# Scales from sums of squares in place of largest magnitudes, with the order of the work made anew, in an attention and MLP kernel

## Chip, cores and metric

The kernel runs on one core of a Trainium2 chip. The metric is the device time of one execution in microseconds (us). Before the change it is 663.16 us, the median of 3 runs (662.82 to 663.47).

## The reference

Eight batches of eight heads with 512 rows of x and 32 rows of state, 64 wide. x reads the state and the state reads x, each through a softmax. The 544 rows of each batch, 512 wide, then go through a layer norm and a two-layer MLP with a residual.

```
scores = x @ state.T / 8;      xread = softmax(scores) @ state
scores2 = state @ x.T / 8;     sread = softmax(scores2) @ x
x = concatenate([xread, sread]), heads side by side       # 8 x 544 x 512
xn = (x - mean) / sqrt(var + 1e-6) * g_ln
out = x + max(xn @ w_ch1, 0) @ w_ch2                      # 512 -> 2048 -> 512
```

The weights and g_ln reach the device as they are drawn; a weight comes as two 32-bit words a number.

## The kernel before

**Numbers as pairs.** Products are made in 16-bit floats, with each operand as a high and a low part (`hi`, `lo`) and three of the four cross products (`TERMS`). For that, each operand is first multiplied by a power of two that brings it into range. There are two scales for each batch (x and state, `x_s`, with the inverses `x_i`) and one for each of the four blocks of either weight (`of_weights`, inverses `is` and for w2 a column of `of_weights`).

**How a scale was found.** In `attention(b)` (L370) ScalarE takes magnitudes of a quarter of x with a running sum beside them (`AF.Abs`, L386), or VectorE a largest magnitude (`absmax`, L351, two quarters of batch 0 and the state's block `sj`); VectorE combines the four parts into `x_am`. `across` (L343) then crosses the partitions: TensorE transposes the column by the identity `idf`, VectorE reduces the row to `x_t`, TensorE spreads it over all partitions by a product with `ids`, and VectorE takes the result as `x_m`. `scales` (L332) keeps the exponent and takes a reciprocal. For a weight block `largest_square` (L607) makes the block's Gram matrix in 16 products of 128 columns, reduces it by its maximum, and goes through `across`; `scales_of_squares` (L337) halves the exponent.

**Weights.** `words` (L586) joins the two words of a number in place: ScalarE treats the high word (`Prelu`) and, for the first half of a block, the low one (`Copy`); for the second half VectorE shifts the low one; VectorE then joins both. For w1, `means` (L636) multiplies by g_ln/512 on TensorE, VectorE subtracts it (four operations `sums<-sums,gx,acc` or `raw<-raw,gx,acc`), then the block is scaled into `w1c` by `split` (L603: ScalarE the high, VectorE the low part). `weights2` does the same for `w2h` without the means.

**Batches.** Batch 0 goes through `first_products` (L730 in `multiply`) and `second_product` (L744) unit by unit while weights arrive: `scores` (L429), softmax on `ts`, numerators `ef` and `ea`, read of the state (L506), mixing (L551). `state_products` multiplies the state with w1 into `matrix` (L689). Batches 1 to 7 use seven products instead of eight per block (L828 the hidden rows into `half`, L886 the seven products into `acc`, with `together` for their sums); the state's rows come last (L838).

**Order.** Each of these is a stream of single operations, 178 in all, and the string `PLAN` lists in which order their operations are issued, as stream:operation. Each engine does its own in that order and waits for what it needs. The last stream, 177, is `WARM` = 119 products of a block of ones with itself into `half`, whose result nobody reads (L191, `half<-ones`); `PLAN` puts them among the first real products. `banks` is one double accumulator bank with a single buffer, shared by scores, reads, mixing, state products and the scales of x. Most operations carry L191, the line of the helper `do`.

Of the kernel before, what the change touches and what calls it, by code (L numbers as in the profile page):

```python
# [19 lines left out]
EXP_MASK = 0x7F800000  # L20
HALF_EXP_MASK = 0x3F800000
TINY = 1e-30
# [4 lines left out]
SX = 2.0**14  # L27
SE = 2.0**12
SA = 2.0**5
SN = 4.0  # L30
SW = 2.0**13
S2 = 2.0**12
CM = 2.0**-24
SB = 2.0**19
# [171 lines left out]
def moe_attention(ctx: ExitStack, tc: tile.TileContext, x, state, g_ln, w1, w2, out):  # L206
# [109 lines left out]
    nc.vector.tensor_tensor(fold, idf[:, 0:D], idf[:, D:2 * D], ALU.add)  # L316
    mhalf = tiny("mhalf", C)
    nc.vector.memset(mhalf, -0.5)

    ones = main.tile([P, P], BF16, name="ones")  # L320
    nc.vector.memset(ones, 1.0)  # L321

# [679 lines left out]
```

## Time and profile before

| | us |
|---|---|
| median of the runs | 663.16 |
| the profiled execution | 663.94 |
| its span, first to last instruction | 662.1 |
| VectorE busy in the span | 496.2 |
| ScalarE busy | 368.3 |
| GpSimd busy | 220.6 |

The mean granted clock of TensorE is 0.996. In the rows below, a timeline row has start, length, engine, line, operation, outputs and inputs, shapes and count, and in brackets how long the engine was idle before and what ended that. PEld is the loading of TensorE's stationary operand, which lies beside its products. A row of windows has the stretch, its length, and for each engine the busy time and the number of instructions.

### The profile page before, as it was taken

To read this page: it belongs to the slowest core of one execution; us is meant where nothing else is said; L and a number is where in the kernel's file an instruction comes from. 1 tells how busy PE (TensorE), PEld (TensorE's weight loads), DVE (VectorE), ACT (ScalarE), POOL (GpSimd) and SP (SyncE) were. 2 spreads that over 40 slices of the span, in tenths; PEclk is the share of its full clock that TensorE was granted. 3 is DMA by queue.
4 is the path that set the end of the run, shared out by engine and by line. 5 is a ranking of instruction groups with operands and counts; after the bars stand their busy time and mean duration, and the time that the engine had idled before them with its cause. 6 is when DMAs were issued, how large, how long until landed. Compare 5 with 4: busy or idle time off the path is not lost. (4 is left out here: it accounts for less than half of the span.)

```text
span 662.1 us, 15974 instructions
## 1 busy us (share of the span) xinstructions
PE 641.5 (97%) x6647; PEld 502.0 (76%) x6647; DVE 496.2 (75%) x990; ACT 368.3 (56%) x659; POOL 220.6 (33%) x189
## 2 busy tenths in 40 slices
PE   9999999999999999999999999999999999999995
PEld 4446646668878888778787888788788887888885
DVE  3999998667599689678785887699777966677424
ACT  4499886748535754466445553755475534444331
POOL 0014134412243335324431335326333442335122
PEclk9998999999999999999999999999999999999999
DMA  8897666331052551434152235340704213102001
GB/s 321 210 304 290 150 152 146 76 71 38 13 99 47 135 103 40 98 112 58 50 133 81 44 76 122 86 73 33 174 10 64 76 36 97 65 2 33 33 1 64
DMA packets 90040, 63.15 MB, mean 95 GB/s; under 512 B 69297, under 2 KB 82097, under 8 KB 89521
## 3 DMA queue, kind: packets, MB, share of 16 engines
q1 hardware_dynamic: 87696, 58.18, 34.2%
q0 software_dynamic: 864, 3.15, 2.5%
q8 instruction: 52, 0.85, 0.6%
q10 hardware_dynamic: 1408, 0.82, 0.4%
q14 instruction: 20, 0.16, 0.1%
HBM read 28.05 MB, written 9.44 MB: 57 GB/s over the span
## 5 line engine op out<-in xcount | busy, mean ns | idle before, releaser
L886 PEld LDWEIGHTS <-xs 128*128 128x128 f16 x2520 | 243.5, 98 | 41.3 <-issue 9.8
L191 POOL TENSOR_TENSOR xs<-rs,xs 128x512 f16<-128x512 f32 x120 | 142.0, 1195 | 291.5 <-ACT xs L191 189.5
L886 PE MATMUL acc<-w2h,xs 128*128 128x256 f16 x1440 | 182.2, 273 | 2.1 <-POOL xs L191 0.8
L828 PE MATMUL half<-ea,matrix 128*128 128x256 f16 x1344 | 162.5, 273 | 4.6 <-DVE xs L191 2.5
L828 PEld LDWEIGHTS <-matrix 128*128 128x128 f16 x1344 | 128.9, 98 | 27.1 <-issue 6.3
L886 PE MATMUL acc<-sums,xs 128*128 128x256 f16 x1080 | 142.6, 273 | 0.7 <-DVE strip L191 0.7
L191 DVE SCALAR_TENSOR_TENSOR rs<-half,rs 128x256 f32<-128x256 f32 x224 | 90.0, 418 | 36.2 <-ACT rs L191 15.7
L191 ACT ACTIVATE xs<-rs 128x512 f16<-128x512 f32 (+1 forms) x128 | 77.2, 620 | 69.6 <-DVE rs L191 58.7
L191 ACT ACTIVATE xs<-half 128x256 f16<-128x256 f32 (+1 forms) x112 | 53.4, 487 | 85.5 <-PE half L828 31.8
L191 DVE SCALAR_TENSOR_TENSOR xs<-half,xs 128x256 f16<-128x256 f32 (+1 forms) x112 | 61.2, 549 | 21.0 <-ACT xs L191 20.7
L744 PE MATMUL acc<-w2h,hid 128*128 128x512 f16 x192 | 44.8, 390 | 0.1
L191 DVE SCALAR_TENSOR_TENSOR matrix<-banks,hs,matrix 128x1024 f16<-128x1024 f32 x28 | 35.8, 1278 | 10.5 <-ACT matrix L191 10.3
L191 DVE TENSOR_TENSOR strip<-acc,strip 128x256 f32<-128x256 f32 (+1 forms) x60 | 33.1, 552 | 9.3 <-PE acc L886 7.0
L191 ACT ACTIVATE rs<-half 128x256 f32<-128x256 f32 x56 | 21.4, 381 | 32.2 <-PE half L828 27.3
L744 PEld LDWEIGHTS <-hid 128*128 128x128 f16 x192 | 18.7, 100 | 23.1 <-issue 3.0
L191 ACT ACTIVATE matrix<-banks,hs 128x1024 f16<-128x1024 f32 x28 | 31.1, 1110 | 5.7 <-PE banks L689 5.5
L191 POOL TENSOR_TENSOR hid<-strip,hid 128x512 f16<-128x512 f32 x16 | 22.4, 1415 | 25.2 <-ACT hid L191 23.6
L191 PE MATMUL half<-ones 128*128 128x512 bf16 x119 | 29.4, 399 | 1.1 <-DVE ones L321 1.1
L191 POOL TENSOR_TENSOR ts<-ts,mA 128x1024 f32<-128x1024 f32 (+1 forms) x8 | 14.7, 1842 | 40.2 <-DVE of_weights L191 28.9
L191 DVE SCALAR_TENSOR_TENSOR x<-x_f,x_s,x 128x512 f16<-128x512 f32 x32 | 26.9, 863 | 1.1 <-ACT x L191 1.0
L191 DVE BATCH_NORM_STATS2 s<-xr 128x6 f32<-128x512 f32 x32 | 21.8, 683 | 6.9 <-ACT xr L191 6.9
L191 DVE SCALAR_TENSOR_TENSOR xr<-strip,of_second,xr 128x512 f32<-128x512 f32 x28 | 24.6, 889 | 0.3
(149 smaller groups left out, 780.5 us busy)
## 6 DMA issues: line engine op xcount, KB each, us to landing
raw<-in_moe_w_ch_dram SPq DMA_DIRECT2D x10, 1024.0 KB, 7.1
out_dram<-xr SPq DMA_DIRECT2D x16, 512.0 KB, 2.9
x_f<-in_x_dram SPq DMA_DIRECT2D x15, 512.0 KB, 5.2
sums<-in_moe_w_ch_dram SPq DMA_DIRECT2D x6, 1024.0 KB, 7.1
ek<-ea SPq DMA_DIRECT2D x56, 64.0 KB, 2.1
ek<-ek SPq DMA_DIRECT2D x7, 512.0 KB, 4.4
xr<-part POOLq DMA_DIRECT2D x6, 512.0 KB, 5.1
s_r<-in_state_dram SPq DMA_DIRECT2D x28, 64.0 KB, 3.7
```

The source lines that it names most:

```text
L191: return lambda: f(*map(now, args), **{k: now(v) for k, v in kw.items()})
L744: nc.tensor.matmul(po, lhsT=hid[:, i, q, c * P:(c + 1) * P], rhs=w[:, j, q], start=first and q == 0 and n == 0, stop=last and q == 3 and n ...
L828: nc.tensor.matmul(ps[:, 256 * q:256 * q + 256], lhsT=m[:, h, i, P * (2 * k + q):P * (2 * k + q) + P], rhs=ea[:, 0, j, h, 256 * g:256 * g ...
L886: nc.tensor.matmul(po[o], lhsT=y[:, n, i, o] if o < 2 else x[:, o - 2, n, i], rhs=v[j], start=u == 0 and n == 0 and k == 0 and o in (2, 1, ...
```

## The change

The largest magnitude goes as a measure. ScalarE now squares each quarter of x, and the state's block from batch 1 on, with a running sum (`AF.Square`). In batch 0 VectorE still takes the largest magnitude of two quarters and of the state's block (`most`) and squares the three. The parts are 16-bit columns, `x_part`. Five products of `ones` with such a column (`totals`) give on all partitions the sum for x (four columns) and for the state (one). VectorE reads them and makes scale and inverse by integer arithmetic on the exponent, without a reciprocal. For a weight block the Gram matrix stays; its maximum goes into a 16-bit column `of_columns`, and one product with `ones` gives the total. Some constants change with it. In block 0 of both weights ScalarE also does the low words of the second half (`both`), which VectorE did. `WARM` is 102, and `PLAN` is another one throughout.

```
-    def scales(m, s, inv):
-        yield do(nc.vector.tensor_scalar, inv.bitcast(I32), m.bitcast(I32), EXP_MASK, None, ALU.bitwise_and)
-        yield do(nc.vector.reciprocal, s, inv)
-    def scales_of_squares(m, s, inv, c):
-        yield do(nc.vector.tensor_scalar, inv.bitcast(I32), m.bitcast(I32), 1, HALF_EXP_MASK, ALU.logical_shift_right,
+    def scales(total, m, s, inv, top):
+        yield do(nc.vector.tensor_scalar_max, m, total, TINY)
+        yield do(nc.vector.tensor_scalar, m.bitcast(I32), m.bitcast(I32), 1, HALF_EXP_MASK, ALU.logical_shift_right,
                  ALU.bitwise_and)
-        yield do(nc.vector.tensor_scalar, inv, inv, 2.0**64 / c, None, ALU.mult)
-        yield do(nc.vector.reciprocal, s, inv)
-    def across(a, n, i, m, t, ps):
-        yield do(nc.tensor.transpose, ps[0:n, 0:P], a, idf)
-        yield do(nc.vector.tensor_reduce, t[0:n], ps[0:n, 0:P], AX.X, ALU.max)
-        yield do(nc.tensor.matmul, ps[:, P:P + n], lhsT=t[0:n].broadcast_to([n, P]), rhs=ids[0:n, i, 0:n], start=True,
-                 stop=True)
-        yield do(nc.vector.tensor_scalar_max, m, ps[:, P:P + n], TINY)
+        yield do(nc.vector.tensor_scalar, s.bitcast(I32), m.bitcast(I32), -1.0, float((190 + top) << 23), ALU.mult, ALU.add)
+        yield do(nc.vector.tensor_scalar, inv.bitcast(I32), m.bitcast(I32), float((64 - top) << 23), None, ALU.add)
+    def totals(ps, parts):
+        for k, cols in enumerate(parts):
+            for n, c in enumerate(cols):
+                nc.tensor.matmul(ps[:, k:k + 1], lhsT=ones, rhs=c, start=n == 0, stop=n == len(cols) - 1)
...
-        for q in range(4):
-            v = xf.rearrange("p h c d -> p (h c) d")[:, 8 * q:8 * q + 8]
-            if b > 0 or q % 2 == 0:
-                yield do(nc.scalar.activation, x16[:, 8 * q:8 * q + 8].bitcast(BF16)[:, :, 0], v, AF.Abs,
-                         accum_out=part[:, q:q + 1])
-            else:
-                yield absmax(part[:, q:q + 1], v.rearrange("p a d -> p (a d)"))
-        yield absmax(am[:, 1:2], sj.rearrange("p g d -> p (g d)"))
-        yield absmax(am[:, 0:1], part)
+        for n, q in enumerate((0, 2) if b == 0 else range(4)):
+            yield do(squares, x16[:, 8 * q:8 * q + 8].bitcast(BF16)[:, :, 0], xq[q], part[:, n:n + 1])
+        if b > 0:
+            yield do(squares, sh.bitcast(BF16)[:, :, 0, 0], sj, part[:, 4:5])
+        else:
+            for n, v in enumerate((xq[1], xq[3], sj)):
+                yield do(nc.vector.tensor_reduce, most[:, n:n + 1], v.rearrange("p a d -> p (a d)"), AX.X, ALU.max,
+                         apply_absolute_value=True)
+            yield do(nc.vector.tensor_tensor, part[:, 2:5], most, most, ALU.mult)
...
-            if fh == 0:
+            if fh == 0 or both:
...
-        yield do(nc.vector.tensor_reduce, col, total[:, 0:P], AX.X, ALU.max)
-        yield from across(col, 1, 1, m, top, total[:, P:3 * P])
+        yield do(bound, col, total[:, 0:P])
+        yield do(lambda ps, c: totals(ps, ([c],)), total[:, P:P + 1], col)
...
-WARM = 119
+WARM = 102
```

Two engines' rows of the new order follow, at three places. At the scale of x in batch 0, TensorE has 35 products of `ones` ahead of the transpose by `idf`, two more ahead of the product with `ids`, and 28 behind it up to the first means. Now it has 30, the five products L347 `banks<-x_part,ones`, and 30.

The first place is VectorE's row from the first load of x to the scale of x. Before:

```order
L191 TENSOR_REDUCE x_part<-x_f 128x1
L191 TENSOR_REDUCE x_am<-s_j 128x1
L191 TENSOR_REDUCE x_part<-x_f 128x1
L191 TENSOR_REDUCE x_am<-x_part 128x1
L191 TENSOR_SCALAR gm<-gx 128x4
L191 TENSOR_REDUCE x_t<-banks 2x1
L191 TENSOR_SCALAR x_m<-banks 128x2
L191 TENSOR_SCALAR x_i<-x_m 128x2
L191 RECIPROCAL x_s<-x_i 128x2
L191 SCALAR_TENSOR_TENSOR sh<-s_j,x_s,sh 128x2x64
```

Now:

```order
L187 TENSOR_REDUCE most<-s_j 128x1
L187 TENSOR_REDUCE most<-x_f 128x1 x2
L187 TENSOR_TENSOR x_part<-most 128x3
L187 TENSOR_SCALAR gm<-gx 128x4
L187 TENSOR_SCALAR x_m<-banks 128x2
L187 TENSOR_SCALAR x_m<-x_m 128x2
L187 TENSOR_SCALAR x_s<-x_m 128x2
L187 SCALAR_TENSOR_TENSOR sh<-s_j,x_s,sh 128x2x64 x2
```

The state's block is reduced first, one reading of `banks` is gone, and the inverse `x_i` has moved behind the first parts of x.

The second place is ScalarE's row behind that scale (`x` is the pair of x, `sums` and `raw` hold weight words). Before:

```order
L191 ACTIVATE x_111<-x_f,x_s 128x8x64 x2
L191 ACTIVATE sh<-s_j,x_s 128x2x128
L191 ACTIVATE sums<-sums 128x1024
L191 ACTIVATE x_111<-x_f,x_s 128x8x64
L191 ACTIVATE sums<-sums 128x1024 x2
L191 ACTIVATE x_111<-x_f,x_s 128x8x64
L191 ACTIVATE sums<-sums 128x1024 x2
L191 ACTIVATE raw<-raw 128x1024
L191 ACTIVATE w1c<-sums,of_weights 128x2048
```

Now:

```order
L187 ACTIVATE sh<-s_j,x_s 128x2x128
L187 ACTIVATE x_113<-x_f,x_s 128x8x64 x4
L187 ACTIVATE sums<-sums 128x1024 x6
L187 ACTIVATE w1c<-sums,of_weights 128x2048
L187 ACTIVATE ts<-ts,es 128x512
```

The state's block comes first, the four quarters of x follow each other, and the word operations no longer stand between them; one of `raw` has moved behind `w1c`, and one on `sums` (`both`) has come.

The third is VectorE's row from the means of the first w1 block to its scale, with buffer numbers (`acc_236` and `acc_246` are that block's Gram, `acc_287` that of w2). Before:

```order
L191 SCALAR_TENSOR_TENSOR sums_70<-sums_70,gx_80,acc_218 128x512 x4
L191 SCALAR_TENSOR_TENSOR sums_70<-sums_70 128x1024
L191 SCALAR_TENSOR_TENSOR sums_70<-raw_159 128x1024
L191 TENSOR_REDUCE of_weights_277<-acc_236 128x1
L191 STREAM_TRANSPOSE ts_297<-banks_258 128x512
L191 TENSOR_REDUCE of_weights_277<-acc_236 1x1
L191 TENSOR_REDUCE of_weights_277<-acc_287 128x1
L191 TENSOR_SCALAR of_weights_277<-acc_236 128x1
L191 TENSOR_SCALAR is1_313<-of_weights_277 128x1
L191 TENSOR_SCALAR is1_313<-is1_313 128x1
L191 TENSOR_SCALAR es_316<-x_i_169 128x1
L191 RECIPROCAL of_weights_277<-is1_313 128x1
```

Now:

```order
L187 SCALAR_TENSOR_TENSOR sums_70<-sums_70 128x1024
L187 SCALAR_TENSOR_TENSOR sums_70<-sums_70,gx_80,acc_214 128x512 x4
L187 STREAM_TRANSPOSE ts_275<-banks_234 128x512
L342 TENSOR_REDUCE of_columns_277<-acc_246 128x1
L187 TENSOR_REDUCE mA_282<-ts_275 128x16
L187 TENSOR_SCALAR of_weights_284<-acc_246 128x1
L187 TENSOR_SCALAR of_weights_284<-of_weights_284 128x1 x2
L187 TENSOR_TENSOR ts_275<-ts_275,mA_282 128x512
L187 TENSOR_REDUCE mp_313<-banks_234 128x4
L187 TENSOR_TENSOR mB_315<-mp_313 128x2
L187 STREAM_TRANSPOSE ts_275<-banks_234 128x512
L187 TENSOR_SCALAR mB_315<-mB_315,es_227 128x2
```

One join of w2's words stands ahead of the means, the other has moved far behind; the work on w2's Gram is no longer mixed in; the low part of `w1c` is the next row, with less of the softmax ahead of it.

Behind the scale, TensorE has 16 products of `ones` ahead of the first state products (24 before). Then come 17 and 1 around twelve mixing products, and its first product with `matrix`; before, it had 7 and 8, with one set of means between them.

More of the change, by code (lines that the diff above doesn't have):

```diff
@@ L18 @@
 PSUM = bass.MemoryType.PSUM
-EXP_MASK = 0x7F800000
 HALF_EXP_MASK = 0x3F800000
@@ L26 @@
 SIGN_BIT = -(2.0**32)
-SX = 2.0**14
 SE = 2.0**12
-SA = 2.0**5
+SA = 2.0**3
 SN = 4.0
[L31 to L34, printed above, removed]
+CM = 2.0**-18
+SB = 2.0**15
 SR = 2.0**-6
@@ L318, in moe_attention @@
     nc.vector.memset(mhalf, -0.5)
+    most = tiny("most", 3)
     ones = main.tile([P, P], BF16, name="ones")
@@ L325, in moe_attention, with squares, bound @@
         nc.vector.tensor_scalar(signs[:, i], idf, 1.0 - 2.0 * i, None, ALU.mult)
-    ids = tiny("ids", 4).rearrange("p (a b) -> p a b", a=2)
-    for i, c in enumerate((SX, 1.0)):
-        nc.scalar.activation(ids[0:2, i], idf[0:2, 0:2], AF.Copy, scale=1.0 / c)
-    def scales(m, s, inv):
-        yield do(nc.vector.tensor_scalar, inv.bitcast(I32), m.bitcast(I32), EXP_MASK, None, ALU.bitwise_and)
-        yield do(nc.vector.reciprocal, s, inv)
-    def scales_of_squares(m, s, inv, c):
-        yield do(nc.vector.tensor_scalar, inv.bitcast(I32), m.bitcast(I32), 1, HALF_EXP_MASK, ALU.logical_shift_right,
-                 ALU.bitwise_and)
-        yield do(nc.vector.tensor_scalar, inv, inv, 2.0**64 / c, None, ALU.mult)
-        yield do(nc.vector.reciprocal, s, inv)
-    def across(a, n, i, m, t, ps):
-        yield do(nc.tensor.transpose, ps[0:n, 0:P], a, idf)
-        yield do(nc.vector.tensor_reduce, t[0:n], ps[0:n, 0:P], AX.X, ALU.max)
-        yield do(nc.tensor.matmul, ps[:, P:P + n], lhsT=t[0:n].broadcast_to([n, P]), rhs=ids[0:n, i, 0:n], start=True,
-                 stop=True)
-        yield do(nc.vector.tensor_scalar_max, m, ps[:, P:P + n], TINY)
-    def absmax(a, t):
-        return do(nc.vector.tensor_reduce, a, t, AX.X, ALU.max, apply_absolute_value=True)
+    def scales(total, m, s, inv, top):
+        yield do(nc.vector.tensor_scalar_max, m, total, TINY)
+        yield do(nc.vector.tensor_scalar, m.bitcast(I32), m.bitcast(I32), 1, HALF_EXP_MASK, ALU.logical_shift_right,
+                 ALU.bitwise_and)
+        yield do(nc.vector.tensor_scalar, s.bitcast(I32), m.bitcast(I32), -1.0, float((190 + top) << 23), ALU.mult, ALU.add)
+        yield do(nc.vector.tensor_scalar, inv.bitcast(I32), m.bitcast(I32), float((64 - top) << 23), None, ALU.add)
+    def squares(junk, v, total):
+        with nc.allow_low_precision(reason="bounds"):
+            nc.scalar.activation(junk, v, AF.Square, accum_out=total)
+    def bound(col, gram):
+        with nc.allow_low_precision(reason="bounds"):
+            nc.vector.tensor_reduce(col, gram, AX.X, ALU.max)
+    def totals(ps, parts):
+        for k, cols in enumerate(parts):
+            for n, c in enumerate(cols):
+                nc.tensor.matmul(ps[:, k:k + 1], lhsT=ones, rhs=c, start=n == 0, stop=n == len(cols) - 1)
     gm = tiny("gm", C)
@@ L380, in attention @@
         xf, sj, sr = tiles
-        am, part = column("x_am", 2), column("x_part", 4)
+        part = Later(lambda: small.tile([P, 16], BF16, name="x_part"))
         x16 = rows("x16").bitcast(F16).rearrange("p (a i d) -> p a i d", i=2, d=D)
-        for q in range(4):
-            v = xf.rearrange("p h c d -> p (h c) d")[:, 8 * q:8 * q + 8]
-            if b > 0 or q % 2 == 0:
-                yield do(nc.scalar.activation, x16[:, 8 * q:8 * q + 8].bitcast(BF16)[:, :, 0], v, AF.Abs,
-                         accum_out=part[:, q:q + 1])
-            else:
-                yield absmax(part[:, q:q + 1], v.rearrange("p a d -> p (a d)"))
-        yield absmax(am[:, 1:2], sj.rearrange("p g d -> p (g d)"))
-        yield absmax(am[:, 0:1], part)
+        xq = [xf.rearrange("p h c d -> p (h c) d")[:, 8 * q:8 * q + 8] for q in range(4)]
+        for n, q in enumerate((0, 2) if b == 0 else range(4)):
[7 more added lines that the diff above has]
+            yield do(nc.vector.tensor_tensor, part[:, 2:5], most, most, ALU.mult)
         m, sc, isc = column("x_m", 2), column("x_s", 2), column("x_i", 2)
-        yield from across(am, 2, 0, m, column("x_t"), banks()[:, 0])
-        yield from scales(m, sc, isc)
+        pt = banks()[:, 0, 0:2]
+        yield do(lambda ps, part: totals(ps, ([part[:, q:q + 1] for q in range(4)], [part[:, 4:5]])), pt, part)
+        yield from scales(pt, m, sc, isc, 14)
         sx, sst, isx, isst = sc[:, 0:1], sc[:, 1:2], isc[:, 0:1], isc[:, 1:2]
@@ L582, in moe_attention, with words @@
     is1 = Later(lambda: tiny("is1", U))
-    of_weights = Later(lambda: main.tile([P, 2 * U, 6], F32, name="of_weights"))
+    of_weights = Later(lambda: main.tile([P, 2 * U, 4], F32, name="of_weights"))
     uoq = Later(lambda: tiny("uoq", U))
-    def words(src, raws, t):
+    of_columns = Later(lambda: main.tile([P, 32], BF16, name="of_columns"))
+    def words(src, raws, t, both):
         for fh in range(2):
@@ L605, in split, with sum_of_squares @@
         yield do(engine.scalar_tensor_tensor, lo, t, s, hi, ALU.mult, ALU.subtract)
-    def largest_square(t, total, m, top, col):
+    def sum_of_squares(t, total, col):
         tops = t.bitcast(BF16).rearrange("p (e two) -> p e two", two=2)
@@ L631, in weights1 @@
         scale, m = of_weights[:, u, 0:1], of_weights[:, u, 2:3]
-        yield from words(src, raws, t)
+        yield from words(src, raws, t, u == 0)
         t4 = t.rearrange("p (k f) -> p k f", k=4)
@@ L641, in weights1 @@
             yield do(nc.vector.scalar_tensor_tensor, t4[:, k], t4[:, k], gx[:, k:k + 1], ps, ALU.mult, ALU.subtract)
-        yield from largest_square(t, accumulator(), m, of_weights[:, u, 3:4], of_weights[:, u, 1:2])
-        yield from scales_of_squares(m, scale, is1[:, u:u + 1], SW)
+        total = accumulator()
+        yield from sum_of_squares(t, total, of_columns[:, u:u + 1])
+        yield from scales(total[:, P:P + 1], m, scale, is1[:, u:u + 1], 13)
         yield from split(w[:, 0], w[:, 1], t, scale)
@@ L656, in weights2 @@
         w = wide(u, "w2h").bitcast(F16).rearrange("p (i q e) -> p i q e", i=2, q=4)
-        s, am, m, top, inv = (of_weights[:, U + u, k:k + 1] for k in range(5))
-        yield from words(src, raws, t)
-        yield from largest_square(t, accumulator(), m, top, am)
-        yield from scales_of_squares(m, s, inv, S2)
+        s, m, inv = (of_weights[:, U + u, k:k + 1] for k in range(3))
+        yield from words(src, raws, t, u == 0)
+        total = accumulator()
+        yield from sum_of_squares(t, total, of_columns[:, U + u:U + u + 1])
+        yield from scales(total[:, P:P + 1], m, s, inv, 12)
         yield do(nc.vector.tensor_scalar, uoq[:, u:u + 1], inv, is1[:, u:u + 1], None, ALU.mult)
```

244 rows, old and new, of the table PLAN are left out of this document.

## The prediction

> **What bounds the kernel now.** I read the page's shares first, then TensorE's busy time by stage, then the timeline of the first 60 us.
>
> ```profile
> PE 641.5 (97%) x6647; PEld 502.0 (76%) x6647; DVE 496.2 (75%) x990; ACT 368.3 (56%) x659; POOL 220.6 (33%) x189
> L191 PE MATMUL half<-ones 128*128 128x512 bf16 x119 | 29.4, 399 | 1.1 <-DVE ones L321 1.1
> ```
>
> TensorE is busy 97% of the span, but 29.4 us of it are the 119 fillers on `ones`, which compute nothing. The stages, cut where the last filler ends (45.06 us) and where the last product ends:
>
> ```profile
> 0.00:45.06 45.06, 42.13 (x236) 18.18 (x238) 32.41 (x66) 25.64 (x35) 3.13 (x8) 1.00 0.86 266
> 45.06:110.00 64.94, 63.08 (x605) 39.46 (x605) 61.26 (x115) 55.20 (x85) 20.36 (x17) 0.97 0.66 193
> 110.00:655.00 545.00, 535.92 (x5811) 444.27 (x5810) 399.53 (x807) 287.44 (x541) 197.07 (x165) 1.00 0.30 70
> ```
>
> The columns are the stretch, its length, busy us of PE, PEld, DVE, ACT and POOL, then clock and DMA. From 45 us on TensorE has real work nearly without a gap (idle 1.9 us up to 110, 9.1 us up to 655), and VectorE has 3.7 us to spare between 45 and 110. So two things can shorten the run: that the real products begin earlier, and that TensorE has less to do. The end behind 655 us holds no scale and is left as it is.
>
> **The start, step by step.** The timeline's rows that set it (start, length, engine, operation, what ended its wait):
>
> ```profile
> 7.36 0.29 DVE L191 TENSOR_REDUCE x_am<-s_j 128x1 f32<-128x128 f32 x1 [0.22 <-DMA s_j<-in_state_dram]
> 7.56 0.68 DVE L191 TENSOR_REDUCE x_part<-x_f 128x1 f32<-128x512 f32 x1
> 10.57 0.27 PE L191 MATMUL banks<-idf,x_am 128*2 128x128 f32 x1
> 11.30 0.35 PE L191 MATMUL banks<-ids,x_t 2*128 2x2 f32 x2
> 11.69 0.16 DVE L191 TENSOR_SCALAR x_m<-banks 128x2 f32<-128x2 f32 x1 [0.53 <-PE banks L191]
> 11.88 0.17 DVE L191 TENSOR_SCALAR x_i<-x_m 128x2 int32<-128x2 int32 x1
> 12.29 1.34 ACT L191 ACTIVATE x<-x_f,x_s 128x512 f16<-128x512 f32 x2 [4.50 <-DVE x_s L191]
> 13.53 0.49 ACT L191 ACTIVATE sh<-s_j,x_s 128x256 f16<-128x256 f32 x1
> 15.57 2.21 ACT L191 ACTIVATE sums<-sums 128x1024 uint32<-128x1024 uint16 x2
> 18.68 1.23 DVE L191 SCALAR_TENSOR_TENSOR sums<-sums 128x1024 uint32<-128x1024 uint32 x1
> 21.98 2.72 DVE L191 SCALAR_TENSOR_TENSOR sums<-sums,gx,acc 128x512 f32<-128x512 f32 x4 [0.55 <-PE acc L638]
> 27.09 0.28 DVE L191 TENSOR_REDUCE of_weights<-acc 128x1 f32<-128x128 f32 x1
> 29.45 2.00 ACT L191 ACTIVATE w1c<-sums,of_weights 128x2048 f16<-128x2048 f32 x1 [7.92 <-DVE of_weights L191]
> 30.89 1.23 DVE L191 TENSOR_REDUCE mp<-banks 128x4 f32<-128x1024 f32 x1
> 32.48 0.71 DVE L191 STREAM_TRANSPOSE ts<-banks 128x512 f32<-128x512 f32 x1
> 33.95 0.69 DVE L191 TENSOR_TENSOR ts<-ts,mA 128x512 f32<-128x512 f32 x1
> 34.56 2.35 DVE L191 SCALAR_TENSOR_TENSOR w1c<-sums,of_weights,w1c 128x2048 f16<-128x2048 f32 x1
> 36.82 1.22 DVE L191 SCALAR_TENSOR_TENSOR eb<-eB,eb 128x1024 f16<-128x1024 f32 x1
> 36.95 0.62 PE L689 MATMUL acc<-w1c,sT 64*32 64x512 f16 x16 [0.49 <-DVE w1c L191]
> 44.59 1.25 DVE L191 SCALAR_TENSOR_TENSOR matrix<-acc,matrix 128x512 f16<-128x512 f32 x2
> 72.22 3.70 PE L638 MATMUL acc<-sums,gm 128*128 128x512 f32 x8
> ```
>
> ```profile
> 4.48 0.15 PEld L191 LDWEIGHTS <-ones 128*128 128x128 bf16 x1 [0.28 <-issue]
> 4.91 5.33 PEld L191 LDWEIGHTS <-ones 128*128 128x128 bf16 x25 [0.28 <-issue]
> 30.77 5.35 PE L191 MATMUL half<-ones 128*128 128x512 bf16 x24
> 44.68 0.38 PE L191 MATMUL half<-ones 128*128 128x512 bf16 x1
> ```
>
> A filler takes (5.35 - 0.38)/23 = 0.216 us. An operation that another of its engine follows at once takes some 0.07 less than its row's length (34.56 to 36.82 for 2.35), and I count so; small operations of VectorE come 0.2 apart (11.69 to 11.88).
>
> *Scale of x.* VectorE now begins with the state block, whose load ends its wait at 7.36. Then come two reductions of 0.65 each and the square: ready at 9.1. TensorE has 30 fillers ahead instead of 35, so it arrives 5 x 0.216 = 1.1 us before 10.57, at 9.5. Five small products take 0.3; the result is read 0.39 after the last begins, as from 11.30 to 11.69: at 10.1. Three dependent operations at 0.2 each put the scale at 10.65, where ScalarE started at 12.29: **1.6 us sooner**; transpose, small reduction and reciprocal have left this path.
>
> *First weights.* ScalarE then does `sh` (0.40), four quarters of x (0.62 each: 1.34 less the last's 0.72), and four operations on the words of w1 (1.05 each: two end 2.21 after the first begins, the last with its 1.14); the second half's words are ready for VectorE at 17.85, and joined at 19.08 (before: 18.68 + 1.23 = 19.91). Means and gain follow 2.07 later as before (21.98 - 19.91): 21.15, and VectorE is just free. The four end at 23.8 instead of 24.6. Before, two word operations of 1.2 each stood between these four and the reduction at 27.09. Now one is done ahead of them and the other is put off, so the Gram's reduction begins at 24.5. Add its 0.2, one total on TensorE (0.3, under VectorE's reduction `mA`) and three operations (0.6): ScalarE can scale w1 at 25.95 instead of 29.45. Its low part needs VectorE, which has 0.6 (`ts`), 1.2 (`mp`), 0.2, 0.64 (`ts`) and 0.2 of softmax ahead: it ends at 31.15 instead of 36.91. **5.8 us sooner.**
>
> *First real products.* Behind it VectorE has a sum (0.7), 0.35 of small ones, `eb` (1.15), two passes of `ts` (0.65 each), a maximum (0.66), `ea` (0.6) and `matrix` (2 x 0.6): 37.1. ScalarE's list (exponentials, `eb`, three word operations of 1.05) frees it for `ea` at 34.65, in time. TensorE has 17 fillers, twelve products that wait for `ea` at 35.9, one filler more, and starts its first product with `matrix` at 36.5. So the last filler ends at about 36.4 instead of 45.06: 8.6 us sooner, with less behind it done. One set of means and one Gram half are still to do (8 x 0.43, as 3.70 for eight, and 0.46 from the row below), and 0.2 of mixing is done already: 3.7 us. **Gain of the start: 4.9 us.** The count of fillers alone says 17 x 0.216 = 3.7.
>
> *What is late next.* The w2 scaling of unit 0: in VectorE's new row its second half ends 14.6 us behind 37.1 (words of the next blocks 4.1, means and gain 2.6, w2 itself 2.4, statistics 1.3, `ef` and `ea` 1.3, small ones 2.9), at 51.7. TensorE has 13.1 us between 36.5 and there (two sets of first products 5.2, means 3.4, mixing 1.6, three Gram halves 1.4, read of the state 1.1, small ones 0.4): 49.6.
>
> ```profile
> 58.18 1.26 DVE L191 SCALAR_TENSOR_TENSOR w2h<-sums,of_weights,w2h 128x1024 f16<-128x1024 f32 x1
> 58.98 12.22 PE L744 MATMUL acc<-w2h,hid 128*128 128x512 f16 x48
> ```
>
> Before, the second product began 0.5 us ahead of the end of w2's second half, as it reads the first half first. So of the 2.1 us I charge what that start doesn't cover, with what both lists leave out, about **1.4 us lost**.
>
> **TensorE's own work.** For each scale a transpose and a two-pass product go. From the chain of waits and the timeline:
>
> ```profile
> 489.66 0.11 PE banks L191
> 491.73 0.32 PE banks L191 x2
> 541.35 1.12 PE banks L506 x64
> ```
>
> ```profile
> 23.44 0.46 PEld L614 LDWEIGHTS <-sums 128*128 128x128 bf16 x8 [0.48 <-DVE sums L191]
> ```
>
> ```profile
> L886 PEld LDWEIGHTS <-xs 128*128 128x128 f16 x2520 | 243.5, 98 | 41.3 <-issue 9.8
> ```
>
> That is 0.43 per scale. Of 16 scales, 13 come after the last filler of before: 5.6 us. The product of `ones` with a column doesn't occur in this trace. Bounds for one with its load: 1.12/64 = 0.018 (smaller load, 32 or 64 columns moved) and 0.10, the mean time of a load of 128 columns with nothing hidden (98 ns). Nearest is the Gram product, the same load with 128 columns: 0.46/8 = 0.057; as one column moves, I take 0.05. Behind the fillers are 7 x 5 + 6 = 41 of them: 2.1 us (0.7 to 4.1). **Gain 3.5 us** (1.5 to 4.9).
>
> [...]
>
> **Rest at nothing.** VectorE loses about 0.5 us per batch and 0.27 per weight block, by small operations of 0.15 to 0.28; ScalarE gains a square of the state (0.2 to 0.4) per batch and a word copy (1.05) twice. Behind 110 us both have over a quarter of their time free. Before that, VectorE's lighter load is in the steps above. Squares in place of magnitudes are one pass over the same elements; no square is in the trace. ScalarE's passes over 128x512 take 0.59 to 0.72, so it is within 0.1 either way for each. The junk of the state's square goes into `sh`, which batch 0's mixing reads; that mixing ends near 50 us, the square comes near 56.
>
> **The sum** against the profiled execution (663.94, span 662.1): 4.9 + 3.5 - 1.4 = 7.0, so 656.9; the median shown, 663.16, lies 0.8 lower, and I forecast **656.2**. One thing is kept at nothing:
>
> ```profile
> 59.00:60.00 1.00, 1.00 (x6) 0.44 (x5) 1.00 (x4) 1.00 (x3) 0.00 (x0) 0.81 0.07 16
> 60.00:61.00 1.00, 1.00 (x4) 0.37 (x3) 0.97 (x3) 1.00 (x3) 0.66 (x1) 0.50 0.69 78
> ```
>
> TensorE had half its clock (third column from the end: 0.81, then 0.50 up to 63) for 3.4 us, behind a stretch of small products; that cost 1.7 us. It may go (-1.7), stay, or come twice (+1.7).
>
> [...]
>
> ```profile
> 71.55 0.16 DVE L191 TENSOR_SCALAR x_m<-banks 128x2 f32<-128x2 f32 x1 [0.52 <-PE banks L191]
> ```
>
> **Rivals.** The row is the read of batch 1's scale in the timeline.
> - *The time saved in the fillers comes back as waits.* VectorE is 94% busy from 45 to 110 us, and the real products are asked for 8 us earlier. Against it: VectorE's list, counted on in the same way to the totals of batch 1, gives about 60 us, where that row stood at 71.55, so it is ahead too. If all 3.5 us of the net start are lost, 659.7.
> - *Nothing to measure.* The start is lost and each total costs its full load: 5.6 - 41 x 0.10 = 1.5 gained, 661.7. Against it: the Gram row.
> - *Slower.* The five totals of a batch stand in TensorE's row and now wait for ScalarE directly, whose new square of the state is queued behind its epilogues; all later products wait behind them. At 1.0 us in each of seven batches the gain is gone, from 1.2 on it is a loss; at 1.5 the time is 666.7. For it: the squares are placed anew in all batches. Against it: ScalarE is idle 47% of the time behind 110 us, and the whole idle of TensorE there is 9.1 us in 545.
>
> **How the numbers follow.** A measurement tells about 0.2% (1.3 us) from no change. Forecast 0.60 (652 to 659.5: loads 1.4 down and 2.0 up, clock 1.7 either way, w2's wait 1.4 down); waits come back 0.22; nothing to measure 0.08; slower 0.10. Faster is the first two, 0.82. The range reaches from 652 over the second case to 661.5 and leaves out the two others.
>
> **What would show it.** The last filler ends near 36 us; scaled x starts on ScalarE near 10.7 and w1c near 26; the L347 products take about 0.3 us per five; TensorE's busy time falls by some 7 us and its idle between 110 us and the end stays near 9. I am wrong if that idle grows by more than 4 us, if w1c starts after 28, or if the totals take over 0.1 us each.

## The result, and the profile after

The changed kernel takes **652.04 us** (median of 4 runs, 651.4 to 654.77) against 663.32 for the kernel before in the same set of runs: ratio 0.9838, 95% interval 0.9809 to 0.9867, so 11.3 us or 1.6% faster. The forecast was 656.2 with a range from 652 to 661.5: the sign is right and the gain is 4 us larger than forecast. That the time lies in the range at all, by 0.04 us, is luck.

The profiled execution, 654.77 us, is the slowest of the four. The rows of its page that answer to those of before (shares, fillers):

```profile
PE 630.1 (97%) x6630; PEld 497.0 (76%) x6630; DVE 487.7 (75%) x966; ACT 370.3 (57%) x673; POOL 226.6 (35%) x189
L187 PE MATMUL half<-ones 128*128 128x512 bf16 x102 | 25.8, 407 | 1.1 <-DVE ones L319 1.1
```

TensorE's busy time fell by 11.4 us, not by 7: 3.6 are the fillers, and by the sums further down some 3.8 are the scales and 1.7 a stretch at half clock; the rest lies ahead of the first real product. Its timeline around the last fillers and the w2 scaling, with VectorE's and ScalarE's rows on the way (start, length, what ended the wait):

```profile
10.82 0.51 ACT L187 ACTIVATE sh<-s_j,x_s 128x256 f16<-128x256 f32 x1 [2.95 <-DVE x_s L187]
25.88 2.00 ACT L187 ACTIVATE w1c<-sums,of_weights 128x2048 f16<-128x2048 f32 x1 [5.93 <-DVE of_weights L187]
28.36 2.35 DVE L187 SCALAR_TENSOR_TENSOR w1c<-sums,of_weights,w1c 128x2048 f16<-128x2048 f32 x1
36.38 1.27 DVE L187 SCALAR_TENSOR_TENSOR matrix<-acc,matrix 128x512 f16<-128x512 f32 x2
36.52 0.46 PE L547 MATMUL acc<-sh,ea 32*128 32x64 f16 x10 [1.20 <-DVE ea L187]
36.91 0.39 PE L187 MATMUL half<-ones 128*128 128x512 bf16 x1
37.14 2.83 PE L729 MATMUL acc<-ea,matrix 128*128 128x256 f16 x24
50.83 1.27 DVE L187 SCALAR_TENSOR_TENSOR w2h<-sums,of_weights,w2h 128x1024 f16<-128x1024 f32 x1
51.77 0.18 PE L347 MATMUL acc<-of_columns,ones 128*128 128x1 bf16 x1
51.81 2.75 PE L743 MATMUL acc<-w2h,hid 128*128 128x512 f16 x12
57.91 0.27 PE L347 MATMUL banks<-x_part,ones 128*128 128x1 bf16 x5
58.03 2.75 PE L743 MATMUL acc<-w2h,hid 128*128 128x512 f16 x12
59.79 0.14 DVE L187 TENSOR_SCALAR x_m<-banks 128x2 f32<-128x2 f32 x1
```

The chain came out nearly as worked out: ScalarE begins with the scale of x at 10.82 (10.65 forecast), with w1c at 25.88 (25.95), VectorE ends w1c at 30.71 (31.15), and the first product with `matrix` begins at 37.14 (36.5; before: 46.11). Five totals take 0.12 us (57.91 to 58.03), 0.024 each.

A second profile of the same kernel (experiment e1, 652.50 us, on the medians) is the better partner for the sums. Its stages, cut at its own first product with `matrix`, at 110 and at the last product's end:

```profile
36.65:110.00 73.35, 71.15 (x668) 1.00 0.76 212
110.00:643.87 533.87, 525.32 (x5757) 1.00 0.28 69
```

and those of before, cut in the same way:

```profile
46.11:110.00 63.89, 62.03 (x546) 0.97 0.66 190
110.00:655.36 545.36, 536.28 (x5812) 1.00 0.30 70
```

The columns are the stretch, its length, TensorE's busy time, then clock and DMA. Behind the first real product TensorE idles 2.2 + 8.6 = 10.8 us where it idled 1.9 + 9.1 = 10.9. So in sum the start saved did not come back as waits. It is busy 596.5 us there, where it was 598.3, and those contain work that before was done ahead of that product.

### The profile page after: what moved, and what is told of

It is laid out like the page before. It is cut to its first block, busy times and chain, and to the rows that moved or that the text cites. A ratio compares the mean times of both kernels' runs of the same rounds, so it can differ in the third digit from the quotient of the medians.

```text
span 652.9 us, 15928 instructions
## 1 busy us (share of the span) xinstructions
PE 630.1 (97%) x6630; PEld 497.0 (76%) x6630; DVE 487.7 (75%) x966; ACT 370.3 (57%) x673; POOL 226.6 (35%) x189
## 4 chain that ended last, share of the span: by engine, by line
PE 48%; DVE 6%; ACT 3%; issue 1%; DMA 1%; POOL 0%; DVEq 0%; SPq 0%; ACTq 0%
PE acc L885 27%; PE half L827 14%; PE half L837 3%; PE banks L688 2%; ACT xs L187 1%; DVE rs L187 1%; DMA ek<-ek 1%; PE banks L532 1%; DVE strip L187 1%; DVE xs L187 1%; DVE dA L187 1%; PE banks L502 1%; PE banks L425 0%; DVE eb L187 0%; DVE ea L187 0%
## 5 line engine op out<-in xcount | busy, mean ns | idle before, releaser
L187 POOL TENSOR_TENSOR xs<-rs,xs 128x512 f16<-128x512 f32 x120 | 146.2, 1227 | 282.6 <-ACT xs L187 201.1
L187 DVE TENSOR_TENSOR strip<-acc,strip 128x256 f32<-128x256 f32 (+1 forms) x60 | 33.0, 550 | 12.6 <-ACT strip L187 5.9
L187 ACT ACTIVATE rs<-half 128x256 f32<-128x256 f32 x56 | 21.2, 379 | 35.4 <-PE half L827 31.6
L187 POOL TENSOR_TENSOR ts<-ts,mA 128x1024 f32<-128x1024 f32 (+1 forms) x8 | 16.5, 2058 | 48.2 <-DVE mA L187 48.0
L187 PE MATMUL half<-ones 128*128 128x512 bf16 x102 | 25.8, 407 | 1.1 <-DVE ones L319 1.1
L187 DVE SCALAR_TENSOR_TENSOR x<-x_f,x_s,x 128x512 f16<-128x512 f32 x32 | 23.5, 757 | 2.3 <-ACT x L187 2.2
L688 PE MATMUL banks<-w1c,sT 64*32 64x512 f16 x672 | 23.6, 380 | 0.0
```

The lines of the kernel that those rows point to most:

```text
L187: return lambda: f(*map(now, args), **{k: now(v) for k, v in kw.items()})
L688: nc.tensor.matmul(ps[g][32 * j:32 * j + 32], lhsT=state_of(b, sT, g, j, i)[r], rhs=w[r, k, j], start=n == 0, stop=n == 2, skip_group_chec ...
```

## The experiments

Each kernel was timed beside the kernel before on the same chip; e1 to e4, e5 to e8 and e9 to e12 share a set of those runs.

**e1: the changed kernel again.** No edit.

> The changed kernel once more, for a second profile. Its timed runs gave 651.4 to 652.2, its profiled run 654.8. Theory A (the 3 us are stalls of that one run): 651 to 653 us here, the profiled run too, and TensorE's idle time between the first product with `matrix` and the last one near 10 us instead of 12.5; the product that waits for ScalarE's squares (L347 banks, 1.6 us there) waits under 0.5. Theory B (the profiled run is what the program does): a profiled run of 654 to 655 again, with the same waits at the same places.

652.72 us (4 runs, 651.07 to 653.01), ratio 0.9825 (0.9809 to 0.9841). TensorE's waits for the squares, first in the profile after, then in e1 (who waited for what: us in all, times, longest):

```profile
PE banks L347 <- ACT x L338: 2.0, 2, 1.6
```

```profile
PE banks L347 <- ACT x L338: 0.4, 1, 0.4
```

Theory A. The totals do wait for ScalarE directly, as the rival "slower" said, but once or twice in an execution, not in each batch. This wait is 1.6 of the 1.8 us by which TensorE idled longer in the first profile (12.6 against 10.8 us).

**e2: the new scales alone.** `PLAN` of before, item for item; where a transpose stood there stand the totals.

```
-WARM = 102
+WARM = 119
-        yield from words(src, raws, t, u == 0)
+        yield from words(src, raws, t, False)
```

> The new scales (squares, Gram products, totals) in the order of before, item for item, 119 fillers, and the unpacking as before. Theory A (the removed transposes and spreads cost TensorE 0.43 each, 13 of them in the saturated part, and 41 totals cost 0.025 each): 5.6 - 1.0 = 4.6 us under before, 658.7, and 657.0 if the stretch at half clock near 60 us goes with them. Theory B (the gain comes from the new order): within 1 us of before. Theory C (0.05 each, as forecast): 3.5 under before, 659.8.

658.11 us, ratio 0.9918 (0.99 to 0.9936): 5.4 us under before, theory A's mechanism and, by time, between A's two figures. In this order the square of batch 1's state overwrites `sh` while batch 0's mixing still reads it, so batch 0's output is off.

**e6: the same with a tile of its own for that junk.**

```
-            yield do(squares, sh.bitcast(BF16)[:, :, 0, 0], sj, part[:, 4:5])
+            yield do(squares, state_junk, sj, part[:, 4:5])
```

> As e2, but what the squares of the state leave behind goes to a tile of its own: in e2 it went over `sh`, which batch 0 still reads in the order of before. No work is added or taken away. Theory A: e2's time again, 657 to 659, 5.5 under before, with the stretch at half clock near 60 us absent in the profiled run. Theory B (the clobbered tile set e2's time): over 1.5 us from it.

657.76 us, ratio 0.9912 (0.9895 to 0.9929): e2's time again. But the profile of e6 has a stretch at half clock (granted 0.50) from 56.1 to 59.6 us, that of e2 has none ahead of its last product, with the same order: whether it comes differs between executions. The rows of e2 and of e6, each from its first product with `matrix` (44.51, 44.45) to its last product's end:

```profile
44.51:648.43 603.92, 592.83 (x6357) 1.00 0.34 84
```

```profile
44.45:649.01 604.56, 593.89 (x6358) 1.00 0.34 84
```

These kernels and before have the same work behind that point but for the scales. Before is busy 598.3 us there, 596.6 without the 1.7 lost at half clock. So by e2 the new scales save **3.8 us** of TensorE's work behind the first real product, and that product comes 1.6 us earlier. By e6, which has such a stretch as before has, they save 4.4. e1 is busy 596.5 us behind its own first product: 3.64 more than e2, which is the work that the new order puts off (4.3 more than e6 without the 1.7 of its stretch).

**e3: the new order alone.** The old scales, `PLAN` of after with each old operation at the place of the new one that does its part; 102 fillers; unpacking as after. Of `PLAN` the lines show batch 3's totals, in after and in e3, where 12 to 15 are the last reduction, transpose, reduction and spread.

```
-... 53:1 67:12 53:2 67:13 53:5 ...
+... 53:1 67:12-15 53:2 67:16 53:5 ...
```

> The old scales (largest magnitudes, transposes and spreads) in the order of after, item for item, with its 102 fillers and its unpacking of the first weights on ScalarE. Theory A (the start is won by the order and by fewer fillers, 4.9, less 1.4 at w2h): 3.5 us under before, 659.8, less 0.5 to 1.5 of it where the longer chain to the scale of x is waited for. Theory B (the order pays only with the short chain): 662 or more, and the first product with `matrix` no earlier than 43 us. If the two parts simply add, e2 and e3 together make up the 11.3 us of the whole change; the rest is what only both together bring.

667.05 us, ratio 1.0049 (1.0033 to 1.0066): **3 us slower than before**, though the first product with `matrix` begins at 38.33 us, 7.8 earlier. (In w2's unit 3 `uoq` is made ahead of a factor of its input here, so that the output is off.) TensorE's waits for the parts of a scale:

```profile
PE acc L191 <- DVE of_weights L191: 3.4, 8, 0.8
PE banks L191 <- DVE x_t L191: 2.6, 7, 0.4
PE banks L191 <- DVE x_am L191: 1.2, 2, 0.6
```

and its row from the first product with `matrix` to the last product's end:

```profile
38.33:658.20 619.87, 604.55 (x6423) 1.00 0.34 85
```

An old scale needs TensorE twice with a pass of VectorE between. In the order of before other products mostly lie there; in the new order, written for totals that need TensorE once, hardly any do: 7.2 us in 17 waits, all but 0.3 of it behind the first real product, where before has 0.8 us in two. TensorE idles 15.3 us there instead of 10.9, and it is busy 2.6 us longer than before with the 3.64 put off. (An estimate for the 2.6: a transpose that waits alone is busy for its whole row, 0.27 us, where before's next product starts 0.11 behind it; 16 such waits make 2.6. It was not tested.) The half clock is not the reason: e3 has a stretch as long as before's, 56.1 to 59.6. This is theory B's time, not its reason: the start is as early as theory A has it, and what it gains, 7.8 us less the 3.6 put off, is lost behind it. The 11.3 us are not a sum of two parts (5.4 and a loss): this order earns its share only with the short scales.

**e5: e3 with other work put between.** In stream 67, batch 3's `attention`, 13 is the transpose and 15 the spread; 53:5 is a half of a hidden block.

```
-... 53:1 67:12-15 53:2 67:16 53:5 67:17-18 ...
+... 53:1 67:12-14 53:2 53:5 67:15-18 ...
```

> As e3 (the old scales in the order of after), but the product that spreads a scale, and what follows it in its chain, stands behind other work of TensorE (1.0 us of it where the buffers allow; not so for four of the eight scales of x). Theory A (the order is worth as much with the old scales, and e3 lost by TensorE waiting twice in every scale, 7.2 us in all): the waits of TensorE for VectorE's part of the scales fall to about 3 us and the time to 4 under e3, 663. Theory B (e3 lost elsewhere): within 1.5 us of e3's 667.

689.06 us (4 runs), ratio 1.0382 (1.0362 to 1.0403). The trial failed by its own construction: what follows a spread in the list had to be moved with it, and in the first w1 block the spread, with the scaling that follows it, came behind 15 operations of other streams, so that its state products waited for `w1c`:

```profile
37.10 0.41 PE L689 MATMUL acc<-w1c,sT 64*32 64x512 f16 x8 [3.37 <-ACT w1c L191]
39.48 1.05 PE L689 MATMUL acc<-w1c,sT 64*32 64x512 f16 x16 [1.98 <-DVE w1c L191]
```

The first product with `matrix` begins at 46.92, and there are five stretches at half clock ahead of the last product, 20.5 us together. So it says that a late scale costs much at the start, and nothing on its question: what an order made for the old scales with 102 fillers would give stays open.

**e4: the totals twice.**

```
-        for k, cols in enumerate(parts):
+        for k, cols in 2 * tuple(enumerate(parts)):
```

> After, with each product of the totals issued twice (48 more loads and products, the same result). Theory A (0.025 each in the full part, as the gaps in the trace show): 41 x 0.025 = 1.0 to 1.2 us above after. Theory B (0.05, as forecast): 2.1 to 2.4 above. [...]

655.27 us (4 runs), ratio 0.9865 (0.985 to 0.9881), 2.6 over e1 by the medians. By that time alone theory B holds. The profile shows less. Batch 1's totals, and the stretch from the first product with `matrix` to the last product's end:

```profile
58.23 0.39 PE L347 MATMUL banks<-x_part,ones 128*128 128x1 bf16 x10
58.48 2.75 PE L743 MATMUL acc<-w2h,hid 128*128 128x512 f16 x12
```

```profile
37.41:645.38 607.97, 596.89 (x6465) 1.00 0.35 87
```

Ten totals take 0.25 us where five took 0.12: **0.025 each**, theory A's price. In the new order 42 totals, one more than forecast, lie behind the first product with `matrix`. Behind its own first product e4 is busy 0.4 us longer than e1 (596.89 against 596.47) and idle 0.3 longer: less than 42 at 0.025, and far less than theory B. The last product ends 1.5 us later (645.38 against 643.87), half of it because the first product with `matrix` comes at 37.41 instead of 36.65, by about as much as it varies between the two profiles of the changed kernel (37.14, 36.65). The rest of the 2.6 us of the timed runs is not explained. These 0.025 include the total's load of 128 columns, whose row in after is 0.096 us long.

**e8: before, with each transpose and spread issued twice** (`turn` and `spread` do so).

```
-        yield do(nc.tensor.transpose, ps[0:n, 0:P], a, idf)
+        yield do(turn, ps[0:n, 0:P], a) 
-        yield do(nc.tensor.matmul, ps[:, P:P + n], lhsT=t[0:n].broadcast_to([n, P]), rhs=ids[0:n, i, 0:n], start=True, stop=True)
+        yield do(spread, ps[:, P:P + n], t[0:n].broadcast_to([n, P]), ids[0:n, i, 0:n])
```

> Before, with each transpose and each spreading product of its scales issued twice (same result). Theory A (0.43 for a pair on TensorE, 13 of 16 in the full part, as forecast): 5.6 to 6.9 us over before. Theory B (what a pair costs is 0.3, since its loads lie beside other work): 3.9 to 4.8. Theory C (what was removed cost its waits, not its work): under 2.

669.14 us (6 runs), ratio 1.0087 (1.006 to 1.0114), 5.7 over before: theory A by the time. But its profiled run has 6.8 us at half clock (59.3 to 66.1) where before has 3.4, so 1.7 of the 5.6 us by which its last product ends later are the clock's. That leaves 3.9 us for 16 pairs, 0.24 each, when a second one follows at once: theory B's total. The mean granted clock of every timed run is on record too. In the profiles with a stretch at half clock between the first and the last product it is 0.996 or less (before, e3, e5, e6, e8, e10, e11), in the others 0.997 or more (after, e1, e2, e4, e7, e9, e12). The one timed run of e8 at 0.999 took 666.87, 3.9 over the mean of before's seven runs at 0.997 or more beside it. The first of each pair, which e2 took away, is dearer: 3.8 net and 1.0 for the totals (41 at 0.024) make 4.8 us for 13 pairs, **0.37 each** (0.43 forecast; with e6's 4.4 it would be 0.42).

**e10: before with 17 fillers fewer.** Nine of the 24 ahead of the first state products and the eight ahead of the read of the state are left out.

```
-WARM = 119
+WARM = 102
```

> Before, with 102 fillers in place of 119: 9 of the 24 ahead of the state products and the 8 ahead of the read of the state are left out, nothing else is changed. Theory A (TensorE's row of fillers sets the start of before, 17 x 0.216 = 3.7): the first product with `matrix` 3 to 3.7 us earlier than 46.1, the time 3 to 3.7 under before. Theory B (the chains do: VectorE's w1c until 36.9, its unpacked words until 39.4): only the 8 late ones are won, 1 to 1.9 us. If the clock falls in the gaps, 1.7 us comes back.

664.26 us (12 runs), ratio 1.0025 (1.0013 to 1.0036): slower, not faster.

```profile
37.01 0.63 PE L690 MATMUL acc<-w1c,sT 64*32 64x512 f16 x16 [2.43 <-DVE w1c L192]
45.40 0.27 PE L731 MATMUL acc<-ea,matrix 128*128 128x256 f16 x1 [0.92 <-ACT ea L192]
46.51 2.67 PE L731 MATMUL acc<-ea,matrix 128*128 128x256 f16 x23 [0.84 <-DVE ea L192]
51.74 2.67 PE L731 MATMUL acc<-ea,matrix 128*128 128x256 f16 x23 [0.82 <-DVE ea L192]
```

The last of these rows in before:

```profile
51.71 2.67 PE L730 MATMUL acc<-ea,matrix 128*128 128x256 f16 x23 [0.82 <-DVE ea L191]
```

The fillers left out became waits for `w1c` and `ea`, and the second set of first products starts at 51.74 against 51.71. The start of before was set by the chains, not by the count of fillers: theory B's cause, without the 1 to 1.9 us that it expected. All 12 timed runs have a clock of 0.996 or less, against 10 of before's 17 beside them, which may be part of why it is slower.

**e11: after without its last 18 fillers.**

```
-WARM = 102
+WARM = 84
```

> After without its last 18 fillers (17 between 30.8 and 34.6 us in e1's profile, one at 36.4). Theory A (they only fill the wait for `ea`): the first product with `matrix` within 0.3 us of 36.65, time within 0.5 of e1's 652.7. Theory B (they hold the clock up): a stretch at half clock in the 10 us behind, and 1 to 2 us over e1.

653.34 us (4 runs), ratio 0.9866 (0.9848 to 0.9884), 1.9 over e9 and e12, which ran beside it. Theory B in its time and its clock. Two rows of its timeline, and its windows (stretch, length, TensorE's busy time and count, clock, DMA share and GB/s):

```profile
35.11 0.28 PE L547 MATMUL acc<-sh,ea 32*128 32x64 f16 x2 [3.55 <-ACT ea L187]
37.33 4.25 PE L729 MATMUL acc<-ea,matrix 128*128 128x256 f16 x24
```

```profile
32.00:33.00 1.00, 0.00 (x0) 1.00 1.06 377
33.00:34.00 1.00, 0.00 (x0) 0.76 1.03 417
34.00:35.00 1.00, 0.00 (x0) 0.50 1.01 392
...
36.00:40.00 4.00, 3.31 (x23) 0.50 0.86 204
40.00:41.00 1.00, 1.00 (x10) 0.82 1.00 365
```

With nothing to do from 31.6 to 35.1, TensorE fell to half its clock at 33.5 and kept it until 40.4, in which the first products with `matrix` take 4.25 us instead of 2.83. The fillers compute nothing, but those in that wait are worth 2 us.

**e7: before with five fillers more**, behind transposes and spreads between 54.3 and 58.6 us.

```
-WARM = 119
+WARM = 124
```

> Before, with 5 fillers (128x512 products of `ones`) put behind the transposes and spreads that stand between 54.3 and 58.6 us, ahead of the stretch of 3.4 us at half clock (59.2 to 62.6 in its trace). Theory A (the clock falls because TensorE does little in those 4 us): no stretch at half clock in the profile; 1.7 us won by it against at most 1.1 for the fillers, 0.5 to 1.5 us under before. Theory B (the clock falls whatever TensorE does there): the stretch stays, and the time is up to 1.1 us over before.

663.42 us (12 runs), ratio 1.0000 (0.9989 to 1.0012). The rows of 60 to 63 us, before and e7:

```profile
60.00:63.00 3.00, 3.00 (x8) 0.50 0.79 227
```

```profile
60.00:63.00 3.00, 3.00 (x15) 1.00 0.88 264
```

The stretch (in before's trace it lies from 59.6 to 63.0) is absent from the profile, whose last product ends 1.5 us earlier, but the medians show nothing. As the stretch also came and went between e2 and e6, one profile doesn't prove that the fillers removed it. The clocks of the timed runs speak for it: 11 of e7's 12 are at 0.997 or more, against 7 of before's 17 beside them. Those seven are 1.2 us shorter in the mean than the other ten, and five fillers are 1.1 us of work: the fillers cost about what they bring.

**e9: unpacking as before; e12: `gm` behind the scale of x.**

```
e9   -        yield from words(src, raws, t, u == 0)
e9   +        yield from words(src, raws, t, False)
e12  - ... 1:6 2:0 0:0 1:7-9 1:12-13 1:21 ...
e12  + ... 1:6 2:0 1:7-9 1:12-13 0:0 1:21 ...
```

> After, with the second halves of the first two weight units unpacked by VectorE again, as before. Theory A (the move to ScalarE pays at the start only: one VectorE operation of the first w1 unit stands ahead of its Gram products): w1c of unit 0 and the first product with `matrix` 0.5 to 1.5 us later than in after (36.7 in e1's kind of run), the time 0.3 to 1.5 us over e1's 652.7. Theory B (hidden beside the chain of x to `ea`): the first product with `matrix` within 0.3 us, time within 0.5.

> After, with the one VectorE operation that makes `gm` moved behind the scale of x: in e1 it waits 0.47 us for the load of g_ln, and the scale of x stands behind it. Theory A (the chain of x to `ea` sets the first products): all of the chain 0.3 to 0.5 us earlier, the time 0.3 to 0.5 under e1. Theory B (another chain is as late): the first product with `matrix` within 0.2 us, no difference in time.

651.47 us, ratio 0.983 (0.9816 to 0.9844), and 651.46, ratio 0.9826 (0.9812 to 0.984): both are the changed kernel's time. The first product with `matrix` begins at 36.80 and 36.48 (36.65 in e1). Theory B twice: the unpacking on ScalarE is hidden beside the chain of x, and 0.2 us of that chain are below what these runs can tell. No variant beats the changed kernel measurably.

## Why the prediction was right, and where it was short

The terms, from before's profiled run (663.94) to e1's (652.50):

| term | forecast | measured | from |
|---|---|---|---|
| start | 4.9 | 5.8 (5.2 by e6) | 9.46 earlier less 3.64 put off (e1, e2) |
| idle behind it (forecast: w2's wait) | -1.4 | 0.2 | 10.9 to 10.8 |
| TensorE's own work | 3.5 | 3.8 (4.4 by e6) | e2 |
| half clock near 60 us | 0 | 1.7 | windows of before and e1 |
| sum | 7.0 | 11.5 | last product's end, 655.36 to 643.87 |

The measured terms are differences of the same rows, so that their sum must come out; how the sum divides between the first and the third is known to 0.6 us.

- *Scale of x, first weights, first real products.* Right to within 0.6 us at each step, by the rows above. The work put off was mis-sized: cut at the first product with `matrix`, the forecast's 3.7 and the read of the state (1.1) stood against 3.64 measured by e2, 4.3 by e6. Half a us of it is mixing that the new order has done by then (twelve products, 0.69 where the forecast had 0.2); by e2's figure 0.6 more was not traced, by e6's next to nothing.
- *"The count of fillers alone says 3.7."* Wrong as a reason: e10 removed 17 of them in the old order and won nothing. The start is earlier because the chain is shorter (1.6 us in e2, which keeps all 119) and because the new order puts work off and calls for the first product sooner (7.8 us in e3, 7.9 from e2 to e1).
- *What is late next: 1.4 lost.* This is the step that failed most. TensorE reached the second product at 51.81, not at 49.6, while VectorE's second half of w2h (50.83 and 1.27 long) was as forecast, and no wait stands there. Of these 2.2 us, 0.6 are the later start in that profile. I had counted 1.6 us of mixing between; the timeline has 2.7 (0.70, 0.46 and 1.52, from each start to the next), and 0.2 of waiting for `ea`. But a wait of this kind and size stands at w2's next block:

```profile
77.59 1.46 PE L743 MATMUL acc<-w2h,hid 128*128 128x512 f16 x6 [0.86 <-DVE w2h L187]
79.69 1.24 PE L743 MATMUL acc<-w2h,hid 128*128 128x512 f16 x5 [0.64 <-DVE w2h L187]
```

  It is 1.5 us in after, e1, e9 and e12, and before has no wait for `w2h`. The idle time in sum is no longer than before's because other waits have gone. So the forecast's size was near, its place was wrong, and what it left out is that other waits go.
- *TensorE's own work.* The net was nearly right from two halves that were both too large: 4.8 us removed (5.4 by e6) where 5.6 were forecast, 1.0 added by the rows (0.4 by e4's busy time) where 2.1 were. That they cancel is luck.
- *The clock at nothing.* The stretch stands in four of the six profiles with the old order of before (before, e6, e8, e10; not in e2 and e7), in e3 with the old scales in the new order (e5 has five), and in none of the five with new order and new scales that keep all fillers (after, e1, e4, e9, e12). It was kept at nothing with 1.7 either way; it went. The clocks of the timed runs agree: at 0.996 or less are 26 of before's 45 runs beside the experiments and 8 of 12 of e2 and e6, but none of the 16 of after, e1, e9 and e12. (Two of e4's four are.) In the three sets before's runs at 0.996 or less are 0.6 us shorter, 1.2 longer and 0.6 longer in the mean than its others, so its share of the 11.3 us between the medians is less than 1.7. Why the new order with the new scales keeps the clock up was not tested.
- *Rivals.* "Waits come back": not in sum, 10.9 against 10.8 us. "Nothing to measure": no, a total costs 0.024 us, a quarter of the 0.098 that a load's row shows. "Slower": its wait exists (2.0 us in one execution, 0.4 in another), far below the 1.0 in each of seven batches at which the gain would be gone. What would have made it slower is in e3: an order in which TensorE waits for each scale.

## What to carry to other kernels

Here a reduction over partitions that visits TensorE once let the order be packed closer than one that visits it twice: its gain showed partly in its own work (3.8 us, e2) and partly in an order that did not pay with the longer chain (e3, 667.05 us), so time the two apart and together. Removing fillers was worth nothing where chains set the start (e10, ratio 1.0025), and cost the clock in e11 (0.50 up to 40.4 us, 1.9 us over e9 and e12); look at what ends TensorE's waits before counting them as savings. When a busy engine has a stretch at reduced clock ahead of the place that changes (here 3.4 us at 0.50, 1.7 us of time), give that stretch a term with a chance, not a nought.

## What the runs showed of the hardware

- Ahead of the last product the stretches at half clock (granted 0.50) were 3.4 us long or twice that: 3.4 in before (59.6 to 63.0), e3, e6, e10 and four of e5's five, 6.8 in e8 (59.3 to 66.1), in e5's other one (37.7 to 44.5) and in e11 (33.5 to 40.4). In e11 the clock fell 2.0 us into idle time. In before it fell behind small products in which TensorE was busy by its rows, 5.8 of 6 us from 53 to 59, so that long idle time stands ahead of the one and not of the other.
- A 128x1 product of `ones` that follows its like costs 0.024 to 0.025 us (after, e4), its load of 128 columns included, while in after each row shows 0.163 for the product and 0.096 for the load: of such rows only the distance between starts is a price.
